# A fused attention and two-layer MLP kernel: second batch's loads gated later, raw weights fetched further ahead, and one VectorE division a pair

## Chip, cores and metric

One core of a Trainium2 chip. The metric is the device time of one execution in microseconds (us), as a median over runs; the profile adds one execution in which every instruction was recorded. Engines are PE (TensorE, with PEld for its weight loads), DVE (VectorE), ACT (ScalarE) and SP (SyncE, which here only issues DMAs).

## What is computed

```python
# q, k, v: (4 batches, 8 heads, 576 positions, 64)
q_d, k_d, v_d = means over groups of 4 positions           # 144 positions
out_d = softmax(q_d @ k_d.T / 8) @ v_d                      # downsampled attention
out_local = softmax(where(|i - j| < 4, q @ k.T / 8, -1e9)) @ v   # band of 7 keys
x = (repeat(out_d, 4) + out_local)                          # -> 2304 tokens x 512
h = x @ w_in;   x = (max(h, 0) + alpha * min(h, 0)) @ w_out         # 512 -> 2048 -> 512
h = x @ w_in2;  out = where(h > 0, h, exp(min(h, 0)) - 1) @ w_out2  # 512 -> 2048 -> 512
```

## The kernel before

**Work and its stages.** All float32 products of the two layers are made of three matmuls on split operands (high times high, high times low, low times high). A batch's 576 positions are two halves of 288 tokens. Layer 1 goes over segments, each a half-batch times a range of the 16 blocks of 128 hidden features: first half 0 of batch 0 with blocks 0 to 9, then half 1 of batch 0 with all 16, then half 0 again with blocks 10 to 15, then the halves of batches 1 to 3; layer 2 follows in groups of 384 tokens. One block of one segment is a *slot*: 12 matmuls into the hidden bank (`mm_in`, called IN below, `bank<-xh,wi` and `bank<-xl,wi` in the profile) and, two slots later, 12 matmuls out of it (`out1`, OUT below, `bank<-gh,wo` and `bank<-gl,wo`). Between them ACT and DVE make `n`, `r`, `gh` and `gl` (`th_elem`). Slots 0 to 9 are the first segment; slot 10 opens the second, slot 26 the third, and slot 32 needs batch 1.

**Weights.** Blocks are items k = 0 to 31, input and output weights in turn (k = 2f and 2f + 1 for block f). Each is loaded as 512 KB of raw 64-bit floats (`load_w`, tiles `rawi` and `rawo`), and turned into a high and a low part by ACT (`raw_a`: `cp<-raw`), two DVE operations (`raw_b`: `cp<-cp`, `cw<-raw,cp`), ACT (`raw_c`: `wi<-cw`) and DVE (`raw_d`: `wi<-cw,wi`). `th_ldw` issues the loads: an item k >= PF waits until item k - PF is converted. The tiles of items 8 to 31 hold batch 0's attention data first, and an item is loaded only when its tile is free: items 8 to 15 after the near-band products `dP,vd` of half 0 (`d_av`), items 16 to 23 after those of half 1 (k = 16 after `vd_142`, 17 after `vd_144`, 18 after `vd_146`, 19 after `vd_148`), items 24 to 31 after batch 0's downsampled attention is done.

**Attention of batches 0 and 1.** `th_pair` loads a head pair (`load_qk`, `load_v`; for batch 1 only after the step named in `GATE`) and sums groups of four on DVE (`sums_qk`, `sums_v`: `sm<-qk`, `sm<-vv`). `th_da` is the downsampled attention: scores on PE (`sd_mm`), copied out and turned into exponentials by ACT (`sd_ev`, `sd_exp`: `P<-bank`, `P<-P,dmx`), maximum, sum and reciprocal on DVE (`dmx`, `dsum`), the division by the sum (`sd_norm`), a transposition (`pt_mm`) and the product with v. In batch 0 a pair is done in two halves (queries 0 to 71, key `(0,)`, and 72 to 143), in batch 1 in one. Batch 1's band comes from full blocks of scores (`th_S`: `bank<-qk`, copied to `ss`), which go to DRAM (`scr`), come back as a diagonal (`s<-scr`), pass a softmax (`th_soft0`), are written as a diagonal into a DRAM buffer of zeros (`p_write`: `pscr<-a`), and are read back as matrices (`p_read`: `pp<-pscr`), transposed and multiplied with v. The zeros of `pscr` are two DMAs of 702 KB from an input.

**What sets the order.** The program is written out by a planner while it is built: every step is a generator (`th_...`) with a priority and a first slot; a clock of the planner's own (`_Clock`) keeps an estimated time of each engine, and a step is emitted when its data are due. So each engine executes one fixed list, in order, and a change of one number or one step reorders the lists of all engines. Where the planner expects a long pause of PE before or between the first slots, it fills it with matmuls on a constant tile (`bank<-warm`).

```python
 42  PB, FB, RB, PF, CS = 1000.0, 300.0, 300.0, 4, 6
 51  GATE = "xc", 0, 0
653                      DVE.tensor_scalar(out=P[:, r, i], in0=P[:, r, i], scalar1=sm[:, r, i], scalar2=None, op0=ALU.mult)
655                      ACT.activation(out=P[:, r, i], in_=P[:, r, i], func=AF.Copy, scale=sm[:, r, i])
1023         yield ("DVE",) if qs == (0,) else ("ACT",)
1235                 if k >= PF:
1236                     yield "key", "cv", 1, k - PF
1538                 SP.dma_start(out=pscr[z][0].rearrange("(q y) -> q y", y=RW + 1), in_=zero_d)
```

`("xc", 0, 0)` is done when slot 0's IN matmuls are issued; `("od", 0, 1)` when the last pair's second half of batch 0's downsampled attention is done; `("w", (1, "o", f))` when item 2f + 1 is converted.

Of the kernel before, what the change touches and what calls it, by code (L numbers as in the profile page):

```python
# [13 lines left out]
ALU = mybir.AluOpType  # L14
# [16 lines left out]
RW = 2 * NU * KW  # L31
SD = S // 4
# [6 lines left out]
QB, QK = 64, 70  # L39
QO = 0, 64, 128, 192, 224  # L40
LIM, EARLY, ECONV, DLA = 1300.0, 700.0, 200.0, 2000.0
PB, FB, RB, PF, CS = 1000.0, 300.0, 300.0, 4, 6
OS, OP, OPS, OSD, OSO, OAV, OX = 5, 15, -8, 6, 0, 10, -5
UD, US, UP, UV = -5, -8, 0, 1
P1, ST1 = 4, 2
# [2 lines left out]
LS = 400.0  # L48
PM, DMG = 300.0, 50.0
PM0, DMG0 = 150.0, 400.0  # L50
GATE = "xc", 0, 0
PN = 1, 5
NB = 2
SDVE = {2: (0,), 3: (0,)}
# [191 lines left out]
def fused_kernel(ctx: ExitStack, tc: tile.TileContext, qk, vt, vl, ql, kl, vb, w_in1, w_out1, alpha,  # L246
# [400 lines left out]

    def sd_norm(key, dve):
        P, sm = st[("P",) + key], st.pop(("ds",) + key)
        for r in range(2):  # L650
            for i in range(len(key[2])):
                if dve:
                    DVE.tensor_scalar(out=P[:, r, i], in0=P[:, r, i], scalar1=sm[:, r, i], scalar2=None, op0=ALU.mult)
                else:
                    ACT.activation(out=P[:, r, i], in_=P[:, r, i], func=AF.Copy, scale=sm[:, r, i])

    def pt_mm(key, bks):
# [94 lines left out]
    def spawn(gen, pri, start=-1, lim=LIM, early=EARLY):  # L752
        threads.append({"g": gen, "p": pri, "s": start, "c": ck.ctx(), "w": None, "l": lim, "e": early})
        threads.sort(key=lambda t: t["p"])

    def finish(*key):
        done[key] = ck.cur["t"]
# [247 lines left out]
    def th_da(b, p, qs):  # L1005
        key = (b, p, qs)
        yield "tok", "P"
        bks = yield "bank", 2
        sd_mm(b, p, qs, bks)
        if b:  # L1010
            put("sm")
        else:
            finish("sdm", p, qs)
        yield ("ACT",)
        sd_ev(key, bks)
        release(bks)
        yield ("DVE",)
        sd_max(key)
        yield ("ACT",)
        sd_exp(key)  # L1020
        yield ("DVE",)
        sd_rec(key)
        yield ("DVE",) if qs == (0,) else ("ACT",)
        sd_norm(key, qs == (0,))
        yield "tok", "pt"
        bks = yield "bank", 2
        pt_mm(key, bks)
        put("P")
        yield ("ACT",)
        pt_ev(key, bks)  # L1030
        release(bks)
        yield "key", "vs", b, p
        bks = yield "bank", 1
        dav_mm(key, bks[0])
        put("pt")
        if b:
            put("vs")
        else:
            finish("dav", p, qs)
        yield ("ACT",)  # L1040
        dav_ev(key, bks[0])
        release(bks)
        finish("od1", b, p, qs)
        if all(("od1", b, z, qs) in done for z in range(NP)):
            finish("od", b, qs[-1])
# [7 lines left out]
    def th_soft0(b, u):  # L1053
        for p in range(NP):
            yield "key", "S", b, p, u
        yield "tok", "s"
        yield ("SP",)
        s_read0(b, u)
        finish("sr", b, u)
        yield "tok", "a"  # L1060
        yield ("DVE",)
        softmax_a((b, u), 1 + u)
        put("s")
        yield ("ACT",)
        softmax_e((b, u))
        yield ("DVE",)
        softmax_b((b, u), 1 + u)
        yield ("SP",)
        p_write(b, u)
        put("a")  # L1070
        finish("pw", b, u)
# [31 lines left out]
    def th_p(b, p, u):  # L1103
        yield "key", "pw", b, u
        yield "tok", "ss"
        yield ("SP",)
        p_read(b, p, u)
        finish("pr", b, p, u)
        yield "tok", "ppT"
        bks = yield "bank", 2  # L1110
        p_tp(b, p, u, bks)
        put("ss")
        yield ("ACT",)
        p_ev(b, p, u, bks)
        release(bks)
        yield "key", "vb", b, u
        yield "key", "od1", b, p, (0, 1) if b else (u,)
        if u:
            yield "key", "xc", b, 0
        elif b:  # L1120
            yield "key", "xc", b - 1, 1 if b > 1 else 2
        bks = yield "bank", 1
        p_av(b, p, u, bks[0])
        put("ppT")
        finish("pav", b, p, u)
        if all(("pav", b, z, u) in done for z in range(NP)):
            put("vl")
        yield ("DVE",)
        p_add(b, p, u, bks[0])
        release(bks)  # L1130
        finish("pa", b, p, u)
        if all(("pa", b, z, u) in done for z in range(NP)):
            finish("xa", b, u)

    def th_x0():
        yield "key", "xc", 0, 1
# [109 lines left out]
    def at(*times):  # L1246
        ck.cur = ck.ctx(max(times) if times else 0.0)
# [178 lines left out]
    with tc.manual_schedule():  # L1426
# [39 lines left out]
        for b in range(1, B):  # L1466
# [6 lines left out]
            if b < NB:  # L1473
                for u in range(2):
                    q = PN[u] + 32 * (b - 1)
# [19 lines left out]
        for s in range(NS1 + NS2):  # L1495
# [21 lines left out]
            key = (ly, "i", f)  # L1517
# [14 lines left out]
            if not s:  # L1532
                finish("xc", 0, 0)
                at(0.0)
                SP.dma_start(out=mask, in_=mask_d)
                for z in (1, 0):
                    at(0.0)
                    SP.dma_start(out=pscr[z][0].rearrange("(q y) -> q y", y=RW + 1), in_=zero_d)
                slot[0] = 0
                spawn(th_x0(), -20)  # L1540
            tm["mm", s] = ck.t["PE"]
            if T7 <= s < NS1:
                finish("fr", (2, "i", f))
# [99 lines left out]
```

## Time and profile before

| what | value |
|---|---|
| median of 3 runs | 959.6 us (959.26 to 961.22) |
| profiled execution, device time | 959.19 us |
| its span, first to last instruction | 957.4 us |
| PE, PEld, DVE, ACT busy | 933.2, 860.6, 564.1, 473.5 us |
| mean granted TensorE clock | 0.986 of full speed |

A line number says little here, since all instructions are issued through one helper (L241); the tiles name them. In a timeline a row is one or several like instructions: start, duration from the first's start to the last's end, engine, line, operation, output and input tiles, shapes, count, and in brackets the idle time before it and what ended it. A table by stage gives for each stretch the busy time of each engine, then the granted clock (1.00 is 2.4 GHz, 0.50 is 1.2 GHz), the share of time in which the DMA engines were busy, and GB/s. `SPq` is the queue of DMA issues.

### The profile page before, as it was taken

The numbers are of one execution on the slowest core, as the hardware profiler recorded it, in microseconds if no ns is written. First come the engines' busy times: TensorE is split into PE (matmuls) and PEld (weight loads), VectorE is DVE, ScalarE is ACT, GpSimd is POOL, SyncE is SP. The second block draws the span as 40 slices with busy tenths as digits, with TensorE's granted clock in tenths as the row PEclk, the third lists the DMA queues.
The fourth block names the chain that finished last, engine by engine and source line by source line (L and its number), as shares of the span: only waits on it lengthen the run. The fifth ranks groups of instructions, "written<-read, shape, count | busy, mean of one in ns | idle before, by whom it ended". The sixth has DMA issues, their size and how long they took to land.

```text
span 957.4 us, 16359 instructions
## 1 busy us (share of the span) xinstructions
PE 933.2 (97%) x6457; PEld 860.6 (90%) x6457; DVE 564.1 (59%) x1202; ACT 473.5 (49%) x1233; POOL 0.2 (0%) x4
## 2 busy tenths in 40 slices
PE   7988998999999999999999999999999999999998
PEld 5777798899999999999999999989999999999997
DVE  6797874535959899899648996233422322322322
ACT  6686884554444562323236686344433433433433
POOL 0000000000000000000000000000000000000000
PEclk9689999999999999999999999999999999999999
DMA  9663744315231423101208930011100200000000
GB/s 284 206 271 120 269 142 53 119 53 173 67 81 46 136 62 92 44 2 60 66 12 317 360 131 34 1 33 67 66 1 1 67 1 1 34 1 1 34 1 33
DMA packets 55874, 84.72 MB, mean 88 GB/s; under 512 B 24594, under 2 KB 35730, under 8 KB 55618
## 3 DMA queue, kind: packets, MB, share of 16 engines
q1 hardware_dynamic: 55798, 83.69, 27.4%
q8 instruction: 50, 0.82, 0.4%
q14 instruction: 26, 0.21, 0.1%
HBM read 69.26 MB, written 15.85 MB: 89 GB/s over the span
## 4 chain that ended last, share of the span: by engine, by line
PE 90%; DMA 4%; ACT 3%; DVE 2%; SPq 1%; issue 1%; ACTq 0%
PE bank L241 90%; DMA qk<-in_qk_dram 2%; ACT P L241 1%; SPq L241 1%; DMA pscr<-a 1%; DMA rawi<-in_w_in_dram 0%; ACT dP L241 0%; ACT cp L241 0%; DVE qk L241 0%; DMA pp<-pscr 0%; DVE dP L241 0%; DVE Dmx L241 0%; DVE wi L241 0%; DVE sm L241 0%; DVE cw L241 0%
## 5 line engine op out<-in xcount | busy, mean ns | idle before, releaser
L241 PE MATMUL bank<-xh,wi 128*128 128x288 f32 x1024 | 242.1, 305 | 3.7 <-DVE wi L241 2.5
L241 ACT ACTIVATE n<-bank 128x288 f32<-128x288 f32 (+1 forms) x224 | 99.4, 444 | 282.6 <-PE bank L241 282.1
L241 PE MATMUL bank<-gh,wo 128*128 128x288 f32 x1024 | 233.2, 300 | 0.1
L241 PE MATMUL bank<-x2h,wi 128*128 128x384 f32 x768 | 211.2, 337 | 0.0
L241 PEld LDWEIGHTS bank<-xh,wi 128*128 128x128 f32 x1024 | 175.9, 190 | 10.2 <-DVE wi L241 3.6
L241 PE MATMUL bank<-wo,gh 128*128 128x512 f32 x576 | 179.2, 392 | 0.0
L241 PEld LDWEIGHTS bank<-gh,wo 128*128 128x128 f32 x1024 | 172.8, 189 | 3.6 <-issue 2.1
L241 DVE SCALAR_TENSOR_TENSOR r<-n,bank 128x384 f32<-128x384 f32 x96 | 53.1, 554 | 208.4 <-ACT n L241 208.4
L241 ACT ACTIVATE gh<-r 128x288 fp32r<-128x288 f32 (+1 forms) x224 | 106.8, 477 | 112.0 <-DVE r L241 111.9
L241 PE MATMUL bank<-xl,wi 128*128 128x288 f32 x512 | 152.9, 299 | 0.4 <-DVE xl L241 0.4
L241 PE MATMUL bank<-gl,wo 128*128 128x288 f32 x512 | 151.2, 295 | 0.0
L241 DVE TENSOR_TENSOR gl<-r,gh 128x288 fp32r<-128x288 f32 (+1 forms) x224 | 111.6, 498 | 63.4 <-ACT gh L241 62.2
L241 PEld LDWEIGHTS bank<-x2h,wi 128*128 128x128 f32 x768 | 140.3, 188 | 3.9
L241 PE MATMUL bank<-x2l,wi 128*128 128x384 f32 x384 | 128.9, 336 | 0.0
L241 PEld LDWEIGHTS bank<-wo,gh 128*128 128x128 f32 x576 | 106.8, 188 | 18.5 <-ACT ys L241 0.4
L241 PE MATMUL bank<-wo,gl 128*128 128x512 f32 x288 | 113.8, 395 | 0.0
L241 DVE SCALAR_TENSOR_TENSOR r<-n,nal,bank 128x288 f32<-128x288 f32 x128 | 65.3, 510 | 62.8 <-ACT n L241 62.3
L241 PEld LDWEIGHTS bank<-xl,wi 128*128 128x128 f32 x512 | 97.7, 191 | 1.1 <-DVE xl L241 1.1
L241 PEld LDWEIGHTS bank<-gl,wo 128*128 128x128 f32 x512 | 96.7, 189 | 0.0
L241 PEld LDWEIGHTS bank<-x2l,wi 128*128 128x128 f32 x384 | 72.1, 188 | 3.8
L241 PEld LDWEIGHTS bank<-wo,gl 128*128 128x128 f32 x288 | 54.0, 188 | 11.5
L241 ACT ACTIVATE n<-n 128x384 f32<-128x384 f32 x96 | 50.5, 526 | 3.0
(99 smaller groups left out, 857.8 us busy)
## 6 DMA issues: line engine op xcount, KB each, us to landing
rawi<-in_w_in_dram SPq DMA_DIRECT2D x32, 512.0 KB
rawo<-in_w_out_dram SPq DMA_DIRECT2D x32, 512.0 KB
qk<-in_qk_dram SPq DMA_DIRECT2D x12, 582.0 KB
yT<-ys SPq DMA_DIRECT2D x32, 144.0 KB
out_dram<-os SPq DMA_DIRECT2D x18, 256.0 KB
vl<-in_vl_dram SPq DMA_DIRECT2D x4, 960.0 KB
vv<-in_vt_dram SPq DMA_DIRECT2D x12, 288.0 KB
kls<-in_kl_dram SPq DMA_DIRECT2D x12, 288.0 KB
```

Source lines behind the costliest of these rows:

```text
L241: return fn(*args, **kw)
```

## The change

- `PF` 4 to 12: an item's load waits for the conversion twelve items back.
- `GATE`: batch 1's loads wait for the end of batch 0's downsampled attention instead of slot 0.
- The two DMAs of zeros into `pscr` leave the place after slot 0 and become a step each (`th_zero`), after the output weights of blocks 5 and 6 are converted; `p_write` waits for its own.
- `sd_norm`: in batches 0 and 1 (b < NB = 2) the division is one DVE `tensor_tensor` over the pair, with the reciprocal broadcast along the keys. Before, half 0 of batch 0 had two DVE `tensor_scalar` operations a pair, half 1 of batch 0 two ACT operations and batch 1 four. Batches 2 and 3 stay on ACT.

```diff
-PB, FB, RB, PF, CS = 1000.0, 300.0, 300.0, 4, 6
+PB, FB, RB, PF, CS = 1000.0, 300.0, 300.0, 12, 6
-GATE = "xc", 0, 0
+GATE = "od", 0, 1
     def sd_norm(key, dve):
         P, sm = st[("P",) + key], st.pop(("ds",) + key)
+        nq = len(key[2])
+        if dve:
+            DVE.tensor_tensor(out=P, in0=P, in1=sm.to_broadcast([72, 2, nq, SD]), op=ALU.mult)
         for r in range(2):
-            for i in range(len(key[2])):
-                if dve:
-                    DVE.tensor_scalar(out=P[:, r, i], in0=P[:, r, i], scalar1=sm[:, r, i], scalar2=None, op0=ALU.mult)
-                else:
+            for i in range(nq):
+                if not dve:
                     ACT.activation(out=P[:, r, i], in_=P[:, r, i], func=AF.Copy, scale=sm[:, r, i])
...
-        yield ("DVE",) if qs == (0,) else ("ACT",)
-        sd_norm(key, qs == (0,))
+        yield ("DVE",) if b < NB else ("ACT",)
+        sd_norm(key, b < NB)
...
         softmax_b((b, u), 1 + u)
+        yield "key", "zero", u
         yield ("SP",)
         p_write(b, u)
...
+    def th_zero(u):
+        yield "key", "w", (1, "o", 5 + u)
+        yield ("SP",)
+        SP.dma_start(out=pscr[u][0].rearrange("(q y) -> q y", y=RW + 1), in_=zero_d)
+        finish("zero", u)
...
-                for z in (1, 0):
-                    at(0.0)
-                    SP.dma_start(out=pscr[z][0].rearrange("(q y) -> q y", y=RW + 1), in_=zero_d)
                 slot[0] = 0
                 spawn(th_x0(), -20)
+                for z in range(2):
+                    spawn(th_zero(z), 0)
```

**Three places in the lists.** First, SP's queue after slot 0, before the change: `pscr` are the zeros, `qk` and `vv` batch 1's first pair, and the raw tiles the items 6 to 10.

```order
L241 DMA xsp<-x 128x1152
L241 DMA mask<-in_mask_dram 128x182
L241 DMA pscr_97<-in_zero_dram 12x14982
L241 DMA pscr_96<-in_zero_dram 12x14982
L241 DMA rawi_648<-in_w_in_dram 128x512
L241 DMA rawo_676<-in_w_out_dram 128x512
L241 DMA qk<-in_qk_dram 128x1164
L241 DMA vv<-in_vt_dram 128x576
L241 DMA rawi_726<-in_w_in_dram 128x512
L241 DMA rawo_754<-in_w_out_dram 128x512
L241 DMA rawi_771<-in_w_in_dram 128x512
```

The same queue with the change, where the zeros and the first pair now stand: `rawi_634` is item 14, `rawi_1052` item 16, `rawi_1225` item 18, `rawo_1284` item 21.

```order
L241 DMA rawi_634<-in_w_in_dram 128x512
L241 DMA rawo_648<-in_w_out_dram 128x512
L241 DMA pscr_96<-in_zero_dram 12x14982
L241 DMA pscr_97<-in_zero_dram 12x14982
L241 DMA rawi_1052<-in_w_in_dram 128x512
L241 DMA rawo_1130<-in_w_out_dram 128x512
L241 DMA rawi_1225<-in_w_in_dram 128x512
L241 DMA qk<-in_qk_dram 128x1164
L241 DMA vv<-in_vt_dram 128x576
L241 DMA rawo_1265<-in_w_out_dram 128x512
L241 DMA rawi_1272<-in_w_in_dram 128x512
L241 DMA rawo_1284<-in_w_out_dram 128x512
```

The zeros and the first pair went back behind items 14 and 18; ahead of `xsp`, in rows not shown, there now stand twelve raw items (0 to 11) where six stood.

Second, PE's list at the product that frees the tile of item 16 (`vd_142`), before the change; `wi_1065` is slot 7's weight.

```order
L241 MATMUL bank_71<-xl,wi_1065 128x288
L241 MATMUL bank_71<-xh,wi_1065 128x288
L241 MATMUL bank_73<-dP_601,vd_142 64x64 x8
L241 MATMUL bank_73<-dP_601,vd_142 64x32 x2
L241 MATMUL bank_72<-dP_631,vd_144 64x64 x8
L241 MATMUL bank_72<-dP_631,vd_144 64x32 x2
```

And with the change, where `wi_986` is slot 6's weight and `wo_829` the output weight of slot 4:

```order
L241 MATMUL bank_70<-xl,wi_986 128x288
L241 MATMUL bank_70<-xh,wi_986 128x288
L241 MATMUL bank_72<-dP_612,vd_142 64x64 x8
L241 MATMUL bank_72<-dP_612,vd_142 64x32 x2
L241 MATMUL bank_66<-gh,wo_829 128x288
L241 MATMUL bank_66<-gl,wo_829 128x288
```

The product moved from the ninth IN matmul of slot 7 to the end of slot 6's: counted in IN and OUT matmuls, 153 stand ahead of it before and 132 with the change, while slot 8 begins after 168 in both.

Third, PE's list at the product that frees the tile of item 18 (`vd_146`), before, inside slot 8's IN matmuls (`wi_1238`):

```order
L241 MATMUL bank_73<-dP_672,vd_146 64x64 x8
L241 MATMUL bank_73<-dP_672,vd_146 64x32 x2
L241 MATMUL bank_70<-xh,wi_1238 128x288
L241 MATMUL bank_70<-xl,wi_1238 128x288
L241 MATMUL bank_70<-xh,wi_1238 128x288 x2
```

And with the change, after OUT matmuls of slot 6 (`wo_1012`):

```order
L241 MATMUL bank_69<-gl,wo_1012 128x288
L241 MATMUL bank_69<-gh,wo_1012 128x288
L241 MATMUL bank_72<-dP_690,vd_146 64x64 x8
L241 MATMUL bank_72<-dP_690,vd_146 64x32 x2
L241 MATMUL bank_73<-ident,P 72x72 x2
L241 MATMUL bank_72<-ident,P 72x72 x2
L241 LDWEIGHTS warm
L241 MATMUL bank_71<-warm 128x256
```

Here 171 IN and OUT matmuls stand ahead of the product before and 192 with the change; slot 9 begins after 192 in both, so no matmul of the layers is left between the product and slot 9, and ten warm matmuls, the two halves of `vd_148`'s products and the first pair's first scores of batch 1 stand there. Batch 1's seventh group of scores stands after 414 IN and OUT matmuls before and 471 now, its first `ident,pp` after 510 and 564.

## Rows read from the trace of the kernel before

**Rows 1.** The page's first part: busy time, share of the span, instructions.

```profile
PE 933.2 (97%) x6457; PEld 860.6 (90%) x6457; DVE 564.1 (59%) x1202; ACT 473.5 (49%) x1233; POOL 0.2 (0%) x4
```

**Rows 2.** Table by stage: stretch, length, PE, PEld, DVE, ACT, POOL busy, clock, DMA, GB/s.

```profile
40.00:60.00 20.00, 16.94 (x150) 13.51 (x149) 18.22 (x46) 16.50 (x63) 0.00 (x0) 0.75 0.99 379
60.00:80.00 20.00, 19.21 (x181) 17.21 (x181) 18.76 (x43) 17.66 (x53) 0.00 (x0) 1.00 0.23 84
...
110.00:158.00 48.00, 47.89 (x431) 43.84 (x430) 36.84 (x83) 38.14 (x114) 0.00 (x0) 1.00 0.46 134
```

**Rows 3.** Timeline of PE, 79 to 108 us.

```profile
79.41 1.36 PE L241 MATMUL bank<-dP,vd 70*64 70x64 f32 x40
...
86.10 1.39 PE L241 MATMUL bank<-warm 128*128 128x256 bf16 x11
88.39 0.40 PE L241 MATMUL bank<-xh,wi 128*128 128x288 f32 x1 [0.90 <-ACT wi L241]
...
89.55 0.40 PE L241 MATMUL bank<-xh,wi 128*128 128x288 f32 x1 [0.62 <-DVE wi L241]
89.88 0.78 PE L241 MATMUL bank<-dP,vd 70*64 70x64 f32 x20
...
99.43 0.53 PE L241 MATMUL bank<-xh,wi 128*128 128x288 f32 x2 [0.84 <-DVE wi L241]
...
101.61 0.38 PE L241 MATMUL bank<-gh,wo 128*128 128x288 f32 x1
...
104.85 0.29 PE L241 MATMUL bank<-xh,wi 128*128 128x288 f32 x1
...
107.94 1.06 PE L241 MATMUL bank<-qk 64*72 64x78 f32 x16 [0.80 <-ACT pt L241]
```

**Rows 4.** Timeline of SP's DMA queue, 78 to 100 us.

```profile
80.22 0.35 SPq L241 DMA_DIRECT2D rawi<-in_w_in_dram  x1
...
90.69 0.33 SPq L241 DMA_DIRECT2D rawi<-in_w_in_dram  x1
```

**Rows 5.** Timeline of ACT, at the landing of items 16 and 18.

```profile
84.07 0.67 ACT L241 ACTIVATE cp<-rawi 128x512 f32<-128x512 f32 x1
...
94.38 0.67 ACT L241 ACTIVATE cp<-rawi 128x512 f32<-128x512 f32 x1 [0.17 <-DMA rawi<-in_w_in_dram]
```

**Rows 6.** Timeline of DVE, at the last conversion step of slots 7, 8 and 9.

```profile
76.81 0.69 DVE L241 SCALAR_TENSOR_TENSOR wi<-cw,wi 128x512 fp32r<-128x512 f32 x1
...
88.81 0.68 DVE L241 SCALAR_TENSOR_TENSOR wi<-cw,wi 128x512 fp32r<-128x512 f32 x1
...
97.00 1.41 DVE L241 TENSOR_REDUCE sm<-qk 128x144 f32<-128x576 f32 x2
...
98.69 0.68 DVE L241 SCALAR_TENSOR_TENSOR wi<-cw,wi 128x512 fp32r<-128x512 f32 x1
```

**Rows 7.** Table by stage, columns as in rows 2, the clock around slot 8.

```profile
90.00:92.00 2.00, 2.00 (x27) 1.96 (x28) 0.55 (x2) 0.00 (x0) 0.00 (x0) 0.77 0.27 20
92.00:94.00 2.00, 2.00 (x12) 1.94 (x11) 0.51 (x1) 1.00 (x4) 0.00 (x0) 0.50 0.63 246
94.00:96.00 2.00, 2.00 (x17) 1.59 (x16) 1.35 (x3) 1.51 (x4) 0.00 (x0) 0.88 0.00 0
```

**Rows 8.** Groups by shape, 20 to 110 us (DVE) and 20 to 170 us (ACT): count, busy us, mean ns.

```profile
L241 DVE TENSOR_TENSOR x<-bank,od 128x288 f32<-128x288 f32 x8 | 3.6, 453 | 2.4 <-PE bank L241 2.3
L241 DVE TENSOR_SCALAR P<-P,dsum 72x144 f32<-72x144 f32 x6 | 1.5, 286 | 0.0
L241 DVE TENSOR_REDUCE dmx<-P 72x4 f32<-72x576 f32 x1 | 0.7, 741 | 0.0
L241 ACT ACTIVATE P<-P,dsum 72x144 f32<-72x144 f32 x24 | 8.2, 405 | 0.5 <-DVE dsum L241 0.5
```

**Rows 9.** Timeline of PE, 135 to 182 us: the two waits in batch 1's and 2's hand-over.

```profile
160.46 0.70 PE L241 MATMUL bank<-ident,pp 72*78 72x72 f32 x8 [2.57 <-DMA pp<-pscr]
...
171.85 0.41 PE L241 MATMUL bank<-ident,sm 128*72 128x128 f32 x2 [1.34 <-DVE sm L241]
```

## The prediction

> **What bounds the kernel now.** I read the page's first part, the tables by stage, and then the timelines of PE, SP, ACT and DVE where PE isn't full. PE is busy 97% of the span [rows 1], so a change can only shorten the time in which it waits or runs at the low clock. The table by stage says where that is: from 110 to 158 us PE is busy 47.89 of 48 us at full clock, but from 40 to 60 us only 16.94 of 20 at a mean clock of 0.75 [rows 2]. In the first 80 us another engine sets the pace: DVE is busy 18.22 and 18.76 of 20 us from 40 to 80 us [rows 2], mostly with raw weights that it converts.
>
> At 86 us it is a chain that sets it. Item 16 (slot 8's input weight) can only be loaded when `vd_142`'s product has freed its tile. That product is one of the two in the row of 79.41 us; the load is issued at 80.22 [rows 4], read by ACT at 84.07 [rows 5], and DVE's last step is done at 88.81 + 0.6 = 89.4 us [rows 6]. PE meanwhile runs eleven warm matmuls, waits twice, and slot 8 gets going at 89.55 [rows 3]. Item 18 repeats it for slot 9: its product at 89.88 [rows 3], load at 90.69 [rows 4], ACT at 94.38 [rows 5], DVE at 98.69 [rows 6], PE at 99.43 [rows 3]. The clock is down to 0.50 from 92 to 94 us [rows 7], after the pause and while the matmuls of slot 8 run. Slot 10 begins at 104.85 us [rows 3]. The last two waits are 2.57 and 1.34 us, near 160 and 172 us [rows 9].
>
> The terms below are in time of the profiled execution: 959.19 us, 0.41 below the median of 959.6, of which 957.4 are span. About 0.2% (1.9 us) is what a measurement of this kernel can tell from no change.
>
> **The change, part by part.**
>
> *Loads further ahead, zeros later (PF, `th_zero`).* Twelve raw items instead of six now stand ahead of `xsp` in SP's queue, and the zeros and batch 1's first pair no longer stand among items 6 to 16. In the stage concerned DMA is full (0.99 from 40 to 60 us), yet DVE is busy 18.22 of 20 us in it [rows 2], so it isn't short of raw data. I cost earlier data at zero up to slot 7. What covers it is DVE's own work; if DVE were faster, DMA would be the next limit. Slot 7's input weight (done at 76.81 + 0.6 = 77.4 us [rows 6]) stays at 77.4.
>
> *Divisions.* Batch 0's half 0 has one TENSOR_TENSOR of 72x288 for two TENSOR_SCALARs of 72x144. A TENSOR_SCALAR takes 286 ns by itself, and the nearest TENSOR_TENSOR (128x288) 453 ns [rows 8]: 0.45 for at most 0.57 us, four times, at most 0.5 us to gain and nothing to lose. The Trainium skill ("VectorE: DVE Perf Modes", "The perf-mode tier table") speaks against the swap: in fp32 a tensor_tensor has half the rate of a tensor_scalar. Taken for the whole instruction, that would double the pair to 1.14 us and add 4 x 0.57 = 2.3 us to the start; the 453 ns of the row don't bear that out, since most of a short instruction isn't its elements. I take 0. In half 1 and in batch 1 the division moves from ACT (2 and 4 operations of 405 ns [rows 8]) to DVE: 4 x 0.45 = 1.8 us more before slot 10, of which two divisions fall before slot 7 and are about paid by one bit operation and one `r` that now stand behind its weight; and 4 x 0.75 = 3.0 us in the second segment (by the 741 ns of a 72x576 reduction, the nearest row [rows 8]; between 453 ns and twice that, 0.9 us).
>
> *The product that frees item 16's tile* now has 132 IN and OUT matmuls ahead of it, slot 7 begins after 144. 24 such matmuls take 104.85 - 101.61 = 3.24 us, 0.135 each [rows 3]. So it ends 12 x 0.135 + 0.4 for one group of transpositions = 2.0 us before slot 7's start at 77.4, at 75.4 us instead of 80.2. From load to DVE's last step the chain took 89.4 - 80.22 = 9.2 us, 3.85 of it to ACT [rows 4 to 6]; it had a sum in it (half the 1.41 us of a pair of sums [rows 6]), and the new list has other short steps there. I take 8.6 us, 84.0 instead of 89.4, with 9.2 (84.6) as the other end. PE gets there by itself after 24 matmuls, 3.2 us, and four groups of small products at some 0.45 us, at 82.4, so the chain still decides and slot 8 resumes at 84.0.
>
> *Item 18.* With the change all of slot 8 and slot 6's OUT stand before `vd_146`: 22 x 0.135 = 3.0, three groups of small products 1.35, the product itself 0.78 [rows 3]: 84.0 + 5.1 = 89.1 us, where it was 90.66. The load is issued 1.5 us earlier, not 5. The chain took 99.43 - 90.69 = 8.7 us; between its steps DVE had a maximum of 0.74 and sums of 1.41 us [rows 6, 8], which now stand behind the conversion. That leaves 7.0 us: slot 9 resumes at 96.2 instead of 99.43, **3.2 us earlier**. The bounds of the chain are 6.3 (all detours gone) and 8.7 us.
>
> *What PE does meanwhile.* Between 89.1 and 96.2 us it has ten warm matmuls (eleven took 1.39 us), `vd_148`'s product (0.78, both [rows 3]), eight score matmuls and two small groups, 3.8 us in all, and idles the rest, 3.3 us. Around slot 8 a shorter pause, eleven warm matmuls in it, was followed by a stretch at 0.50 [rows 3, 7]. I expect the same here, as long as there (a mean of 0.77, 0.50 and 0.88 over three stretches of 2 us is 0.9 + 2.0 + 0.5 = 3.4 us at 0.50), which costs half, **1.7 us lost**, since slot 9's matmuls now wait for nothing else. The bounds are 0 and 1.7. The old stretch was covered by slot 9's wait and gives nothing back.
>
> *Slot 10.* 36 matmuls and the first sums' transposition: 96.2 + 4.9 + 0.4 + 1.7 = 103.2, less 0.2 for the three IN matmuls that slot 9 can do before its low part is there: 103.0 against 104.85, **1.85 us gained**. In slot 10 PE waited 0.80 us for `pt` of batch 1's first pair [rows 3], which now comes some hundred matmuls later: **0.80 gained**.
>
> *Batch 1 later (GATE).* DMA: its first pair now follows item 18 in the queue and delays items 19 to 21, which ACT meets before slot 10's `xh`; slot 10 has 6 us for that, so I cost it at 0. DVE: three pairs' sums, three of 0.7 us a pair (1.41 for two [rows 6]), 6.3 us in all, and 1.2 us of maxima and reciprocals move from before to behind slot 10, with the 3.0 us of divisions. In 110 to 158 us DVE is busy 36.84 of 48 us [rows 2]; with 10.5 more, in a stretch that some 4 us of moved PE work make longer, 47 of 52, 91%. It fits, with little left. The hand-over of the band through DRAM is the same chain as before: from the seventh group of scores to the first `ident,pp` there are 93 IN and OUT matmuls instead of 96, so the wait of 2.57 us [rows 9] grows by 3 x 0.135 = **0.4 us lost**. The load of batch 2's first pair now stands ahead of the second `pscr` write in SP's queue, but its transposition is due 27 matmuls after the first `ident,pp` instead of 66; I leave its 1.34 us [rows 9].
>
> Sum: -1.85 - 0.80 + 0.4 = -2.25, so 959.19 - 2.2 = **957.0 us**.
>
> **Rivals.**
>
> *A: the conversion still sets the pace (no change).* Item 18's tile comes free only 1.5 us earlier. If its chain stays at 8.7 us, because items 16 and 17 with their divisions still occupy DVE, 1.7 of the gain goes: 958.7. For it: DVE is over 90% busy to 80 us [rows 2]. Against it: it was busy only 0.55 and 0.51 of 2 us after 90 us [rows 7].
>
> *B: DVE becomes the bound of the second segment (slower).* Place: slots 10 to 22. Its 91% there leave 5 us; each microsecond of dependent waiting beyond those is one of PE's, since `gl` of each slot goes through DVE. DVE was busy 36.84 and idle 11.2 us [rows 2]; if as much as that must stay idle because it waits for ACT and PE, it is 11.2 - 5 = 6 us late, and with the gains kept 957.0 + 6 = 963.0; at half of it 960. The point from which it decides is an idle need of 5 us. Against it: `gl` has two slots of slack.
>
> *C: the clock holds (faster).* If the warm matmuls keep it at 1.00 after 89 us, 1.7 us come back, and if the hand-over's softmax is shortened by the four ACT divisions (24 took 8.2 us [rows 8], so 1.4) that leave ACT, the wait of 2.57 falls by about 1: 959.19 - 2.25 - 2.7 = 954.3. The Trainium skill ("TensorE: Matmul & The Clock Gate", "Loop structure matters more than you think") says that matmuls behind a long wait for a DMA run cold, which is against this rival; rows 7 agree (0.50 after the pause at 86 to 89 us).
>
> *D: the change does nothing of what it says.* Items 8 to 31 wait for their tiles whatever PF is, so PF = 12 could be idle; the lists show that all else moved, so this gives the same time as A.
>
> **How the numbers follow.** Forecast 0.36, A with D 0.24, B 0.22, C 0.18. The forecast lies 0.23% below; with its unknowns I give two thirds of it to faster, one third to the same. A is the same for 0.17 and faster for 0.07; B is slower for 0.20 and the same for 0.02; C is faster. That makes faster 0.24 + 0.07 + 0.18 = 0.49, same 0.12 + 0.17 + 0.02 = 0.31, slower 0.20. The range goes from 952.8 (C, with the remaining 1.5 us of the hand-over wait gone too) to 961.2 (B at two thirds).
>
> **What would show it.** In the profile after, right: item 16's load near 75 us and item 18's near 89; slot 9 resumed near 96; slot 10 at 103; no pause in 110 to 158 us; a low clock near 91 to 96 us. Wrong: slot 7's weight away from 77 by over 2 us (then the first stage wasn't DVE's alone), waits of PE for `gl` or `r` between slots 10 and 26 (B), a wait above 4 us ahead of `ident,pp`, or a clock at 1.00 throughout after 60 us (C).

## The result, and the profile after

The changed kernel takes 966.93 us (median of 4 runs, 965.15 to 968.41), the one before 959.43 (4 runs, 957.87 to 961.22): a ratio of 1.0084, with a 95% interval of 1.0068 to 1.0100 (ratios and their intervals are over all executions; the quotient of the two medians can differ from them by some 0.001, and is 1.0078 here). It is 7.5 us slower, where 2.2 us faster was forecast. The profiled execution took 968.41 us, 9.22 more than that of before. The page's first part and a table by stage of the changed kernel (stretch, length, busy PE, PEld, DVE, ACT, POOL, clock, DMA share, GB/s):

```profile
PE 936.3 (97%) x6451; PEld 863.3 (89%) x6451; DVE 568.1 (59%) x1206; ACT 466.8 (48%) x1209; POOL 0.2 (0%) x4
```

```profile
0.00:60.00 60.00, 47.66 (x437) 35.30 (x438) 42.36 (x108) 39.10 (x154) 0.20 (x4) 0.77 0.83 273
60.00:80.00 20.00, 17.48 (x158) 15.28 (x158) 18.90 (x45) 16.27 (x51) 0.00 (x0) 1.00 0.03 4
80.00:112.00 32.00, 25.85 (x251) 22.19 (x250) 21.22 (x48) 17.35 (x50) 0.00 (x0) 0.89 0.59 198
112.00:155.00 43.00, 42.67 (x383) 39.26 (x384) 37.80 (x78) 33.58 (x96) 0.00 (x0) 1.00 0.54 185
155.00:220.00 65.00, 60.82 (x573) 56.32 (x572) 29.70 (x72) 32.81 (x106) 0.00 (x0) 0.95 0.36 79
```

The kernel before in two of these stretches:

```profile
80.00:112.00 32.00, 27.52 (x268) 23.05 (x265) 24.98 (x54) 23.40 (x69) 0.00 (x0) 0.95 0.65 226
...
155.00:220.00 65.00, 61.07 (x587) 56.54 (x588) 26.77 (x62) 32.80 (x100) 0.00 (x0) 1.00 0.32 83
```

PE is full from 112 to 155 us, as before [rows 2]; it loses time around slots 6 to 9 and in the *hand-over*, the way of batch 1's band through DRAM to PE with the start of batch 2's attention (155 to 220 us). Its timeline there, first one row of the kernel before (slot 6's weight), then the changed kernel:

```profile
73.05 0.53 PE L241 MATMUL bank<-xh,wi 128*128 128x288 f32 x2 [0.79 <-DVE wi L241]
```

```profile
75.89 0.40 PE L241 MATMUL bank<-xh,wi 128*128 128x288 f32 x1 [0.46 <-DVE wi L241]
...
81.56 0.30 PE L241 MATMUL bank<-xh,wi 128*128 128x288 f32 x1
...
88.32 0.40 PE L241 MATMUL bank<-xh,wi 128*128 128x288 f32 x1 [1.07 <-DVE wi L241]
...
101.56 1.32 PE L241 MATMUL bank<-qk 64*72 64x78 f32 x16 [4.05 <-DMA qk<-in_qk_dram]
102.81 0.61 PE L241 MATMUL bank<-xh,wi 128*128 128x288 f32 x1
...
109.35 0.29 PE L241 MATMUL bank<-xh,wi 128*128 128x288 f32 x1
...
172.64 0.70 PE L241 MATMUL bank<-ident,pp 72*78 72x72 f32 x8 [1.88 <-DMA pp<-pscr]
...
187.72 0.44 PE L241 MATMUL bank<-ident,sm 128*72 128x128 f32 x2 [2.31 <-DVE x L241]
```

Slot 6 waits for its weight at 75.89, slot 7 begins at 81.56 (77.4 before), slot 8 resumes at 88.32 (89.55 [rows 3]), slot 9 begins at 102.81 (before, it begins at 98.06 and goes on, after a wait, at 99.43), slot 10 at 109.35 (104.85). The second wait of the hand-over, 1.34 us before [rows 9], is 2.31. It is another one: before, the first pair of batch 2 waits there (the matmul stands behind 576 IN and OUT matmuls), now the second pair (behind 621). What led to it stands in SP's queue and in DVE's list:

```profile
78.87 0.34 SPq L241 DMA_DIRECT2D rawi<-in_w_in_dram  x1
...
94.06 0.33 SPq L241 DMA_DIRECT2D rawi<-in_w_in_dram  x1
94.43 1.86 SPq L241 DMA_DIRECT2D qk<-in_qk_dram  x1
...
171.41 0.36 SPq L241 DMA_DIRECT2D qk<-in_qk_dram  x1
171.81 0.43 SPq L241 DMA_DIRECT2D vv<-in_vt_dram  x1
172.29 0.40 SPq L241 DMA_DIRECT2D pscr<-a  x1
173.37 3.29 SPq L241 DMA_DIRECT2D pp<-pscr  x2
176.71 0.36 SPq L241 DMA_DIRECT2D qk<-in_qk_dram  x1
```

```profile
100.72 0.69 DVE L241 SCALAR_TENSOR_TENSOR wi<-cw,wi 128x512 fp32r<-128x512 f32 x1 [0.76 <-ACT wi L241]
...
184.38 1.42 DVE L241 TENSOR_REDUCE sm<-qk 128x144 f32<-128x576 f32 x2 [2.82 <-DMA qk<-in_qk_dram]
185.71 0.74 DVE L241 TENSOR_REDUCE dmx<-P 72x4 f32<-72x576 f32 x1
...
186.56 0.74 DVE L241 TENSOR_REDUCE sm<-vv 128x144 f32<-128x576 f32 x1
187.22 0.81 DVE L241 TENSOR_TENSOR x<-bank,od 128x288 f32<-128x288 f32 x2
```

Batch 2's first pair is loaded ahead of the second `pscr` write (171.41), its second pair only behind two reads of `pp` (176.71). Before, that load was issued here:

```profile
163.74 0.53 SPq L241 DMA_DIRECT2D qk<-in_qk_dram  x1
```

DVE comes to the second pair's sums, waits 2.82 us for that load, and does what stands behind them in its list only then. PE's `ident,sm` of 187.72 transposes the sum of the pair's v (`sm<-vv`, done at 187.31), and needs a bank that the first of the two `x<-bank,od` frees (done at 187.67). So the pair's own late sums hold PE for nearly all of the 2.31 us, and the bank adds 0.36. The clock falls behind the three long waits of the timeline (4.05, 1.88 and 2.31 us):

```profile
102.00:104.00 2.00, 2.00 (x19) 1.85 (x17) 0.86 (x2) 1.12 (x3) 0.00 (x0) 0.50 0.99 387
104.00:106.00 2.00, 2.00 (x10) 2.00 (x10) 1.70 (x3) 1.32 (x3) 0.00 (x0) 0.50 0.89 321
...
174.00:176.00 2.00, 2.00 (x16) 2.00 (x14) 1.12 (x2) 0.98 (x3) 0.00 (x0) 0.58 1.01 294
176.00:178.00 2.00, 2.00 (x11) 2.00 (x11) 1.41 (x3) 0.00 (x0) 0.00 (x0) 0.57 0.87 37
...
188.00:190.00 2.00, 2.00 (x14) 1.94 (x12) 0.89 (x4) 1.79 (x8) 0.00 (x0) 0.50 0.04 8
```

### The profile page after: what moved, and what is told of

Read it like the earlier page. It is cut to its first block, busy times and chain, and to the rows that moved or that the text cites. A ratio compares the mean times of both kernels' runs of the same rounds, so it can differ in the third digit from the quotient of the medians.

```text
span 966.6 us, 16345 instructions
## 1 busy us (share of the span) xinstructions
PE 936.3 (97%) x6451; PEld 863.3 (89%) x6451; DVE 568.1 (59%) x1206; ACT 466.8 (48%) x1209; POOL 0.2 (0%) x4
## 4 chain that ended last, share of the span: by engine, by line
PE 87%; DMA 5%; DVE 3%; ACT 3%; issue 1%; SPq 1%; ACTq 0%; DVEq 0%
PE bank L241 87%; DMA qk<-in_qk_dram 3%; ACT dP L241 1%; ACT P L241 1%; DVE cw L241 1%; DMA pscr<-a 1%; SPq L241 1%; ACT cp L241 0%; DMA rawo<-in_w_out_dram 0%; DVE dmx L241 0%; DVE cp L241 0%; DVE wi L241 0%; DMA pp<-pscr 0%; DVE r L241 0%; ACT wi L241 0%
## 5 line engine op out<-in xcount | busy, mean ns | idle before, releaser
L241 PE MATMUL bank<-gh,wo 128*128 128x288 f32 x1024 | 236.2, 302 | 0.4 <-ACT ys L241 0.2
L241 PEld LDWEIGHTS bank<-xh,wi 128*128 128x128 f32 x1024 | 177.1, 192 | 12.4 <-DVE wi L241 5.0
L241 PEld LDWEIGHTS bank<-wo,gh 128*128 128x128 f32 x576 | 106.9, 188 | 18.4 <-ACT ys L241 0.4
```

Of the source, the lines that this page charges most:

```text
L241: return fn(*args, **kw)
```

## The experiments

I call the *loss* of a stretch what PE is idle in it plus half of its busy time at the low clock, from tables by stage in windows of 1 us. The ratio is to the kernel before on the same chip, over the same set of runs, whose median was 959.63 us beside runs 1 to 4, 957.48 beside 5 to 8, 958.13 beside 9 to 12 and 957.62 beside 13 to 16.

| kernel | ratio (95%) | loss to 60 us | 60 to 112 | 112 to 155 | 155 to 220 |
|---|---|---|---|---|---|
| before | 1 | 21.9 | 7.0 | 0.0 | 3.9 |
| the change | 1.0084 (1.0068 to 1.0100) | 24.7 | 10.9 | 0.3 | 7.6 |
| 5: the change again | 1.0080 (1.0064 to 1.0096) | 22.0 | 10.0 | 0.0 | 8.0 |
| 1: GATE back | 1.0007 (0.9991 to 1.0023) | 22.6 | 5.0 | 1.5 | 3.4 |
| 2: division back | 1.0030 (1.0015 to 1.0045) | 19.7 | 10.1 | 0.0 | 6.8 |
| 3: PF back | 1.0044 (1.0029 to 1.0059) | 24.9 | 10.0 | 1.9 | 0.7 |
| 4: division alone | 1.0002 (0.9990 to 1.0015) | 23.2 | 10.1 | 3.0 | 0.0 |
| 6: batch 2 early | 1.0031 (1.0019 to 1.0044) | 20.8 | 10.4 | 0.0 | 1.7 |
| 7: gate one pair earlier | 1.0058 (1.0040 to 1.0075) | 21.4 | 15.4 | 0.0 | 5.3 |
| 8: GATE alone | 1.0007 (0.9993 to 1.0021) | 21.9 | 7.4 | 2.5 | 0.3 |
| 9: second pair earlier | 1.0059 (1.0037 to 1.0080) | 18.4 | 12.6 | 0.1 | 5.5 |
| 10: 6 with scores behind slot 9 | 1.0031 (1.0010 to 1.0051) | 24.8 | 15.7 | 0.4 | 0.7 |
| 11: 1 with batch 2 early | 0.9992 (0.9975 to 1.0008) | 23.0 | 6.4 | 0.5 | 0.3 |
| 12: zeros back | 1.0107 (1.0079 to 1.0134) | 17.8 | 12.8 | 0.2 | 7.5 |
| 13: before, batch 2 early | 1.0003 (0.9989 to 1.0017) | 20.8 | 8.3 | 0.0 | 3.7 |
| 14: 13 with GATE | 1.0033 (1.0013 to 1.0053) | 24.5 | 7.5 | 3.6 | 0.1 |
| 15: 6 with an earlier gate | 1.0068 (1.0049 to 1.0087) | 24.3 | 7.2 | 0.3 | 3.5 |
| 16: 11 again | 0.9993 (0.9981 to 1.0006) | 19.9 | 5.4 | 0.5 | 0.8 |

A loss is one profiled execution's, a ratio that of all executions. Up to 60 us the loss goes from 17.8 to 24.9 us with no order in it (the change and its repeat: 24.7 and 22.0), so nothing is read from that column, and elsewhere only what recurs.

**1 to 4: one part taken back, or alone.**

```diff
 1: -GATE = "od", 0, 1
    +GATE = "xc", 0, 0
 2: -        yield ("DVE",) if b < NB else ("ACT",)
    +        yield ("DVE",) if qs == (0,) else ("ACT",)
    ...
 3: -PB, FB, RB, PF, CS = 1000.0, 300.0, 300.0, 12, 6
    +PB, FB, RB, PF, CS = 1000.0, 300.0, 300.0, 4, 6
```

Run 4 is the kernel before with the new `sd_norm` and its two calls.

> The changed kernel with GATE back at ("xc", 0, 0); PF = 12, the later zeros and the new divisions stay. The median of the change is 966.9 us, that of the kernel before 959.4. Summed over the two profiled executions, PE loses 10.7 us more (idle, and half of its busy time at the low clock) with the change: 4.5 of it up to 80 us, 2.2 from 80 to 112 us (slot 9), 4.0 from 112 to 200 us (the hand-over). Theory G (batch 1's loads come too late: slot 9 stands behind batch 1's first scores, and the hand-over and batch 2's loads collide): the last two go, 960 to 961.5 us, first `ident,pp` without a low clock behind it. Theory P (the far loads starve the first stage): stays at 964 to 967. Theory D (the divisions on DVE hold up the conversions): stays at 964 to 967.

> The changed kernel with the divisions as before (TENSOR_SCALAR in half 0, ACT elsewhere); GATE, PF = 12 and the later zeros stay. Theory D: 960 to 963 us, with slot 6's input weight back at 73 us (75.8 with the change). Theories G and P: 965.5 to 968, slot 6's weight stays at 75 or later, the pause ahead of slot 9 stays at 4 us and the clock falls behind the hand-over.

> The changed kernel with PF back at 4; GATE, the later zeros and the new divisions stay. Theory P: the 4.5 us up to 80 us go, 961 to 963 us, slot 6's weight at 73 us. Theory G: the start may gain, the pause ahead of slot 9 stays near 4 us, and the whole at 964 to 968; but here the first `ident,pp` stands behind 447 IN and OUT matmuls instead of 564, so that the hand-over no longer meets batch 2's loads, and if G's loss lies in that meeting alone, it is 960 to 963 as well. Theory D: 965 to 968.

> The kernel before with the new divisions alone. Theory D: slower than before, 961 to 965 us. Theories G and P: no slower than 960; and since the product that frees item 16's tile stands behind 108 IN and OUT matmuls here instead of 153, slot 8 no longer waits and 956 to 958.5 us are possible, if the first stage leaves DVE the time.

GATE back takes all of the loss (959.55 us), as theory G said, a little more than it said. But the divisions back (962.18, within theory D's range) and PF back (962.71, within theory P's) take about half of it each, and the divisions alone (959.81) cost nothing, which is against D: the cost is one of GATE together with the others. PF alone and the later zeros alone were not run. In run 3 the loss of the hand-over was nearly gone (0.7), as in the second case that theory G had for it, and yet the total fell only by half. In run 2 slot 6's weight came earlier, as D said, with a wait of PE that ended at 72.42 us, and the pause ahead of slot 9 was 3.01; in run 3 it came at 76.81, not at the 73 that P said.

**5 to 8: the place of the loss.**

```diff
 6: -g0 + 2 * p + OPS if b > 1 else ST1 + ST2 * p
    +g0 + 2 * p + (-16 if b == 2 else OPS) if b > 1 else ST1 + ST2 * p
 7: -GATE = "od", 0, 1
    +GATE = "dav", 2, (1,)
```

Run 5 is the change itself, run 8 the kernel before with `GATE = "od", 0, 1`.

> The changed kernel once more, unedited, for a second trace and a closer median. Theory H (the hand-over of batch 1's band comes so late that it meets batch 2's first loads): 965 to 968 us, with the wait for `pp` and the one near 188 us (2.31 us, for the second pair's qk) there again. Rival K (the profile of the change caught a bad clock): the waits recur, but the 3.4 us that the low clock cost from 155 to 200 us don't, and the median comes down to 962 to 964.

> The changed kernel with batch 2's pairs allowed 8 slots earlier (start -16 instead of -8), so that its first two loads stand ahead of both `pscr` writes; the lists up to 450 IN and OUT matmuls don't change. Theory H: the loss from 155 to 220 us (7.6 us in the change's trace, 3.9 before) goes down to 4 or less and the kernel to 962 to 964 us. Theory S (what is lost is lost up to slot 9: 81.6 instead of 77.4 us at slot 7, 102.8 instead of 98.1 at slot 9, and never made good): 966 to 968.

> The changed kernel with GATE at the third pair's second half of the downsampled attention instead of the last pair's. Item 18's tile is freed behind the same 192 IN and OUT matmuls and slot 9 is as late as with the change, but the first `ident,pp` stands behind 507 matmuls instead of 564, and both `pscr` writes stand ahead of batch 2's loads again, as before. Theory H: 960 to 963 us, the wait near 188 us gone. Theory S: 965 to 968.

> The kernel before with GATE alone changed; the first `ident,pp` stands behind 456 IN and OUT matmuls here (510 before, 564 with the whole change). Theory H: no later hand-over, so no loss there: 959 to 961 us. Rival G0 (the late gate costs by itself, at slot 9, whatever else is done): 962 to 965, with a wait for qk of 3 us or more ahead of slot 9.

The repeat executes the same lists, and has both waits of the hand-over again:

```profile
168.83 0.70 PE L241 MATMUL bank<-ident,pp 72*78 72x72 f32 x8 [1.49 <-DMA pp<-pscr]
...
183.86 0.64 PE L241 MATMUL bank<-ident,sm 128*72 128x128 f32 x2 [3.23 <-DVE x L241]
```

and 2.84 us lost at the low clock (3.40 in the first trace), against rival K. With batch 2 early the ratio goes from 1.0080 to 1.0031 in the same set of runs, 4.25 us (964.87 to 960.62), and the loss from 155 to 220 us from 7.6 and 8.0 to 1.7. SP's queue and PE of that run:

```profile
154.99 0.72 SPq L241 DMA_DIRECT2D qk<-in_qk_dram  x1
...
158.57 0.36 SPq L241 DMA_DIRECT2D qk<-in_qk_dram  x1
...
162.94 2.67 SPq L241 DMA_DIRECT2D pscr<-a  x1
```

```profile
175.12 0.67 PE L241 MATMUL bank<-ident,pp 72*78 72x72 f32 x8 [1.73 <-DMA pp<-pscr]
```

Both loads are out before the first `pscr` write, the wait for `pp` is as long as in the change, and it is PE's only one there. So the hand-over carries about half of the loss. With batch 2 early it loses less than even in the kernel before (1.7 against 3.9), so not all of the 4.25 us is what the change added there; by the traces that is 3.7 and 4.1 us. Run 7 is a miss: 963.55 us, 1.0058, with a wait of 1.81 left in the hand-over, and slot 9's weight only used at 105.07. GATE alone is level, although PE waits 3.04 us for qk ahead of slot 9, which rival G0 took for the sign of a loss: its hand-over loses 0.3 instead of 3.9, and 2.5 us go elsewhere, in waits of 1.31 and 1.15 us at 116 and 130 us.

**9: two DMAs past one read.**

```diff
-g0 + 2 * p + OPS if b > 1 else ST1 + ST2 * p
+g0 + (0 if (b, p) == (2, 1) else 2 * p) + OPS if b > 1 else ST1 + ST2 * p
```

> The changed kernel with batch 2's second pair allowed two slots earlier. The lists of PE, DVE and ACT are those of the change, word for word; on SP's alone the pair's qk and v pass one read of `pp`, which in the change's trace keeps them for 2.9 us (the second read issued at 176.3, qk at 176.71). Theory H in its closest form (DVE waits in its list for that qk, and behind it stands the sum `x<-bank,od` that frees the bank for PE's `ident,sm` at 187.7): the wait of 2.31 us there (3.23 in the second trace) shrinks to under 0.5, with it the low clock behind it, and the kernel comes to 4 to 5.5 us over the one before instead of 7.5. Rival H2 (the pair's load is slow because it shares the DMA engines with the first pair and `pp`, wherever it stands): the wait stays over 1.5 us and the kernel within 1.5 us of the change.

SP's queue, then DVE and PE:

```profile
168.94 3.06 SPq L241 DMA_DIRECT2D pp<-pscr  x1
172.04 0.36 SPq L241 DMA_DIRECT2D qk<-in_qk_dram  x1
```

```profile
178.69 1.41 DVE L241 TENSOR_REDUCE sm<-qk 128x144 f32<-128x576 f32 x2 [3.10 <-DMA qk<-in_qk_dram]
...
181.54 0.81 DVE L241 TENSOR_TENSOR x<-bank,od 128x288 f32<-128x288 f32 x2
```

```profile
182.04 0.64 PE L241 MATMUL bank<-ident,sm 128*72 128x128 f32 x2 [2.23 <-DVE x L241]
```

Between the two theories: the wait stayed, as H2 has it, and the median is 5 us over before, as H has it, but at 1.0059 it is not told apart from the change's with certainty. The first read alone held SP for 3.06 us, so the load came hardly earlier; it took 6.65 us from issue to DVE's sum (7.67 and 7.27 in the two traces of the change; the first pair's load 4 us). Why it is slow was not tested. The chain from qk through DVE's list to PE is there, but its last link is not the one that theory H names: the v sum that `ident,sm` reads ended at 181.62, the sum that frees the bank at 181.98. That moving this one load alone would save the wait is not shown.

**10 and 11: slot 9.**

```diff
10: +        if (b, p) == (1, 0):
    +            yield "key", "in9"
    ...
    +            if s == 9:
    +                finish("in9")
```

(the first in `th_S`, the second behind slot 9's `mm_in`; with run 6's edit). Run 11 is run 1 with run 6's edit.

> The changed kernel with batch 2's pairs 8 slots earlier, as in the run before, which was 3.1 us over the kernel before, and batch 1's first score groups held until slot 9's IN matmuls are issued. Theory Q (slot 9 waits for batch 1's first qk, which stands behind item 18's load): slot 9 starts 2 us or more earlier, the kernel 0 to 1 us over the one before. Rival I (item 18's conversion ends as late: last step done at 101.4 us in the change's trace, the qk's scores began at 101.56): slot 9 as late as with the change, only the order of the wait changes, and the kernel stays 2.5 to 3.5 us over the one before.

> The changed kernel with GATE back and batch 2's pairs 8 slots earlier. With GATE back alone it was level with the kernel before (ratio 1.0007); its trace lost 3.4 us from 155 to 220 us. If theory H also holds here, up to 2 us of these go: 1 to 2.5 us faster than the kernel before. If not, level within 1 us; slower if the earlier loads take DVE's or DMA's time from the second segment.

In run 10 PE waits at least as long, for item 18's weight instead of qk, with the ratio of run 6, as rival I said (the trace is of the longest of its twelve executions):

```profile
102.81 0.40 PE L241 MATMUL bank<-xh,wi 128*128 128x288 f32 x1 [2.81 <-ACT wi L241]
105.90 0.85 PE L241 MATMUL bank<-xh,wi 128*128 128x288 f32 x2 [2.56 <-DVE wi L241]
```

Runs 6 and 11 differ in GATE alone: 1.0031 and 0.9992, 0.4% or some 3.7 us, and from 60 to 112 us a loss of 10.4 against 6.4 (10.0 to 15.7 in the change, its repeat and the four variants with the same gate, PF and divisions; 5.0 to 6.4 in the three runs with GATE back). The stretch from 80 to 112 us, run 6 first, then run 11:

```profile
80.00:112.00 32.00, 27.29 (x257) 23.91 (x257) 22.17 (x49) 19.34 (x55) 0.00 (x0) 0.89 0.64 218
```

```profile
80.00:112.00 32.00, 28.22 (x283) 23.85 (x283) 25.79 (x58) 22.56 (x66) 0.00 (x0) 1.00 0.59 205
```

With GATE back, batch 1's scores and sums stand between slots 8 and 9, no wait there is over 1.1 us, and the clock stays at 1.00; with the late gate PE waits 3.3 us at once and the clock falls. That this is where the 0.4% lies is argued from the losses and not shown: the trace of run 6 is of its shortest execution (958.41 us) and that of run 11 of its longest (958.71), so the two differ by 0.3 us in total, and run 8 has such a wait and is level.

**12: the zeros at their old place.** Edit: the two DMAs back after slot 0, `th_zero` and its key out.

> The changed kernel with the zeros of `pscr` back at their place after slot 0; PE's, DVE's and ACT's lists are those of the change. Costed at nothing: 6.5 to 8.5 us over the kernel before, as the change. Rival Z (the zeros' 1.4 MB ahead of items 12 to 15 delay these): over 9 us. Rival Z2 (the zeros where the change has them delay items 16 to 19): under 5.5 us.

1.0107, over the 9 us of rival Z, but the interval (1.0079 to 1.0134) meets the change's: by the point values the later zeros save 2.2 to 2.6 us, but no saving at all is possible too. There is no sign that they cost.

**13 to 16: what the late gate moves.**

> The kernel before with batch 2's pairs 8 slots earlier, nothing else. Its trace lost 3.9 us in the hand-over (2.57 and 1.34). Theory H in general (a load that the hand-over doesn't meet saves the wait behind it): the 1.34 us go and perhaps part of the 2.57, 1 to 3 us faster than the kernel before. Rival E (batch 2's earlier PE and DVE work only moves the pause elsewhere): within 1 us.

> The kernel before with GATE changed and batch 2's pairs 8 slots earlier. Theory F (the late gate takes batch 1's work, 4.3 us of PE before slot 9 in the kernel before and 1.6 with the gate, out of the stretch where PE waits for weights and puts it where PE is full; GATE alone came out level only because its hand-over lost 0.3 instead of 3.9 us): with batch 2 early there is nothing left to gain in the hand-over, so this is 1.5 to 3 us slower than the run of the kernel before with batch 2 early. Rival F0 (the work moved is free): level with that run within 1 us.

> The changed kernel with batch 2's pairs 8 slots earlier and GATE at the second pair's scores of half 1, so that 6.6 us of batch 1's PE work stand ahead of slot 10 (5.1 before, 2.9 with the change), 1.9 of them ahead of slot 9 (4.3 and 1.6). With GATE as in the change and batch 2 early it was 3.1 us over the kernel before, with GATE back and batch 2 early 0.8 under. Theory F: between the two, 0.5 under to 1.5 over. Rival C (batch 1's sums on DVE hold up item 18's conversion, as in the run with the gate one pair earlier, where slot 9 began past 105 us): 3 to 5 us over.

> The changed kernel with GATE back and batch 2's pairs 8 slots earlier, once more, unedited. Measured at a ratio of 0.9992 (0.9975 to 1.0008) before. If it is faster than the kernel before at all, again 0.996 to 0.9995; if it is level, 0.999 to 1.001.

Run 13 is the kernel before with run 6's edit, run 14 also has GATE, run 15 is run 6 with `GATE = "sdm", 1, (1,)`. Run 13 is level (rival E): the 1.34 us are gone, but a wait of 2.00 stays and the clock falls behind it, which it had not done before. Run 14 is 0.3% slower than run 13 by the ratios and 1.6 us by the medians, the size that theory F gave, though the two intervals still meet. It has two waits that run 13 doesn't have:

```profile
115.81 0.40 PE L241 MATMUL bank<-gh,wo 128*128 128x288 f32 x1 [1.32 <-ACT ys L241]
```

```profile
153.41 0.67 PE L241 MATMUL bank<-ident,pp 72*78 72x72 f32 x8 [2.29 <-DMA pp<-pscr]
```

But run 13 loses as much in its own hand-over: from 112 to 220 us it is 3.7 us in both, and from 60 to 112 us 7.5 in run 14 and 8.3 in run 13. So these two traces don't show where the 0.3% lies, and theory F is not shown. Run 15 is a miss for F: 1.0068, slot 9 resumed only at 103.81 us, which is rival C's sign, and the median is 6.3 us over, more than C said; the trace taken (span 959.7 us) doesn't show where its median of 963.95 comes from. Run 16 repeats run 11's 0.9992 with 0.9993. Twelve runs each don't tell that from no change, so no version is shown to beat the kernel before.

## Why the prediction was wrong

The sign is wrong, and the time lies beyond the range. By the prediction's steps, in the profiled execution:

*Slot 7's weight stays at 77.4.* **Failed**: slot 7 begins at 81.56, 80.2 in the repeat. Slot 6 already waits for its weight until 75.89 (73.05 before). DVE wasn't alone in setting the pace: up to 75.9 us it is busy 57.2 us with the change and 59.6 before, so it waited 2.4 us more (1.2 in the repeat). Why is not settled; three waits for PE's bank ahead of `x<-bank,od` are 3.3 us together (1.6 before). Each of runs 1 to 4 has slot 7 at 79.6 to 82.5 us, so taking one part back doesn't restore it, and one part is enough to move it: with the divisions alone it begins at 81.75 (run 4), with GATE alone at 79.94 (run 8), and both are level in time.

*Divisions.* Right: 453 ns for 72x288 and 751 for 72x576, forecast 0.45 and 0.75. The 1.14 us that the prediction worked out from the rule of the Trainium skill ("VectorE: DVE Perf Modes", "The perf-mode tier table") for the case that it holds for the whole instruction are not there; the row of 453 ns was the better guide.

*Items 16 and 18.* The distances nearly held, the start didn't. Item 16's load is issued 2.7 us before slot 7 (2.0 forecast), its chain took 88.32 - 78.87 = 9.5 us (8.6 forecast, 9.2 the other end). Item 18's load is issued at 94.06 instead of 89.1; from there to the end of DVE's last step at 101.4 are 7.3 us. The forecast was 7.0, where the prediction's own rows leave 8.7 - 0.74 - 1.41 = 6.6; rival A's 8.7 is not there. Behind the load PE had a group of scores to do (16 matmuls, the prediction counted eight), 1.25 us, that I counted as filling the pause. But they wait for batch 1's qk, which stands behind item 18 in SP's queue (94.43), and came only when the weight was there too. In the repeat they did fill it: they ran from 98.28 to 99.53 us, and the weight was done at 100.03. Slot 9 begins at 102.81 instead of 96.2 (99.53 in the repeat). The low clock behind it cost 2.25 us; 1.7 were forecast.

*Slot 10, 1.85 gained.* **Failed twice.** It begins 4.5 us later in this execution, 1.9 in the repeat. Its size is uncertain: PE's list up to here is the same in runs 5, 6, 9 and 12, where slot 10 begins at 105.8 to 107.7 us, and run 13 has the list of before and begins it at 106.27 instead of 104.85. None of these comes near the 103.0 that was forecast. And the sum took slot 10's start for progress, though the change leaves work of batch 1 undone there that the kernel before has done: one group of scores, one transposition of sums, one of `P` and the eight matmuls of one `bank<-sm`. From the start of such a group to that of the next they take 0.71, 0.13, 0.46 and 0.64 us, 1.9 in all. I named "some 4 us of moved PE work" in the DVE term and charged none of it to PE, in a stretch where PE is full. The 0.80 of slot 10 did go.

*Hand-over.* **Failed, and it is the largest part that recurs.** I forecast 0.4 more on the wait for `pp`; that wait fell, to 1.88. The other I left at 1.34, having looked at batch 2's first pair only: the second pair's load went behind a `pscr` write and two reads, 13 us later than before, while its transposition is due after 621 IN and OUT matmuls instead of 633. Loss there: 7.6 us for 3.9, 8.0 in the repeat.

The account of these two executions closes: 4.5 (slot 10) + 1.9 (work moved behind it) - 1.16 (two waits in slot 10 that are gone) + 0.3 (112 to 155 us) + 3.7 (hand-over) = 9.2 us, their difference. For the repeat the same sum is 1.9 + 1.9 - 1.16 + 0.0 + 4.1 = 6.7 us where it took 5.7 us more, so the sum is good to about 1 us, and of its terms the hand-over's is the one that stays. By all executions, run 6 gives the hand-over up to 0.5% and runs 6 and 11 give GATE 0.4% beside it; where PE loses the latter is not shown.

Rival B had the sign and not the mechanism: DVE was busy 37.80 of 43 us from 112 to 155, 88%, and PE 42.67. Rival C's clock didn't hold: it fell in more places than before. D is out, since PF alone moves the result from 1.0044 to 1.0080 (runs 3 and 5) and GATE alone from 0.9992 to 1.0031 (runs 11 and 6). Open: what delays slot 6, where half of the cost lies, and why GATE, level in the kernel before (run 8), costs what it does with PF and the divisions; runs 2 and 3 show only that the hand-over's place depends on all three (its first `ident,pp` stands behind 609 and 447 matmuls there, behind 489 with GATE back and behind 564 in the change).

## What to carry to other kernels

Work that is taken out of a stretch in which an engine waits has to be charged in full where it goes; an earlier start of the next stage is no gain until both versions have done the same work. When a queue is reordered, follow every transfer in it to its due time, the second of a pair too, and look in the waiting engine's list for what stands behind the wait: here the sum that PE needed stood behind the sums of a late load, and the one that freed its bank behind that. The engine that a wait is put down to can itself be held by a DMA. Parts that cost nothing alone, here GATE and the divisions, can cost 0.8% together with others, so they are to be tried both ways, alone and taken out of the whole. And before a term is read from one pair of traces, the same lists are to be traced twice: slot 10's 4.5 us were 1.9 the second time.

## What was unexpected of the hardware

Among waits of about 2 us, the length doesn't tell whether the clock falls. Behind 2.57 us [rows 9] it stayed at 1.00 in the kernel before, behind 1.88 us at 172.64 it was 0.58 and 0.57 from 174 to 178 us in the changed one, and in run 13 a wait of 2.00 us was followed by 0.50. The clock of the kernel before, then wait and clock of run 13:

```profile
160.00:162.00 2.00, 1.54 (x17) 1.53 (x18) 0.00 (x0) 0.71 (x2) 0.00 (x0) 1.00 0.91 68
162.00:164.00 2.00, 2.00 (x21) 2.00 (x20) 0.95 (x2) 1.44 (x4) 0.00 (x0) 1.00 0.36 38
```

```profile
164.35 0.75 PE L241 MATMUL bank<-ident,pp 72*78 72x72 f32 x8 [2.00 <-ACT P L241]
```

```profile
166.00:168.00 2.00, 2.00 (x11) 1.94 (x10) 1.93 (x7) 2.00 (x10) 0.00 (x0) 0.50 0.60 107
```

All of these are waits ahead of the first `ident,pp`, and so are 2.47 us in run 1, with 0.50 from 158 to 160 us behind it, and 2.29 us in run 14, with 1.00. The Trainium skill ("TensorE: Matmul & The Clock Gate", "Loop structure matters more than you think") says that matmuls behind a long wait for a DMA run cold; 0.50 behind the 4.05 us agrees, and the waits of 1.9 to 2.6 us go both ways.

One read of `pp` kept SP's queue for 3.06 us, where most issues take 0.3 to 0.4 (run 9). And one set of lists gives traces whose low clock up to 60 us costs 12.4 us (the change) and 8.4 us (its repeat): effects of 2 to 3 us were only to be seen in medians, and in what recurs.
